# The opening of a fused attention and FFN kernel: image lines of the first two pairs summed on VectorE, first value products set behind the last image line, fp32 dummies in place of fp16 ones

## The chip, the cores and the metric

The kernel runs on one core of a Trainium2 chip. The metric is the device time of one execution in microseconds (us); a profile's span leaves out about 1.8 us of it.

## The reference

```python
B, C, Hh, Ww = (4, 128, 384, 32)              # q: B x 12288 x 128, kv: an image B x 384 x 32 x 128
kv_pool = kv.reshape(B, H//4, 4, W//4, 4, C).mean(axis=(2, 4))
k = v = kv_pool.reshape(B, -1, C) @ w_sr      # 768 keys per batch
a = softmax(q @ k.T / sqrt(C));  x = a @ v    # then a gated FFN, d_ff = 1536:
out = (maximum(x @ w_gate, 0) * (x @ w_val)) @ w_out
```

## The kernel before

The main loop takes 512 queries (a tile) at a time and keeps TensorE full: scores, value products, the two FFN projections and the output product of different tiles are interleaved. In front of it stands an opening that has to pool and project the first batch's image while it arrives. The image comes as three pairs of key chunks with four lines (512 KB each) per pair. A line is pooled by being transposed into one PSUM bank, where the transposes add up, or by being added to another line on VectorE.

```python
def fill(n):                                   # dummies, to raise TensorE's clock (full at 7.66 us)
    for _ in range(n):
        nc.tensor.matmul(idle, ident16, filler, start=True, stop=True)
fill(8)
def values(k, jc, half): ...                   # 2 products of 129 columns into x_banks[k, half]
def attend(k, pair): ...                       # values for both chunks and halves of a pair: 8 products
def turn_add(chunk, lines, first=False): ...   # fp32 transposes adding into kv_Ts[chunk]
def add_lines(pair): ...                       # VectorE: line 0 + line 1, 1024 elements per partition
...
for dh in range(3):                            # pair 0: all four lines on TensorE
    for h in range(2):
        turn_add(h, line(0, dh, h), first=dh == 0)
...
nc.gpsimd.tensor_copy(gate, line(2, 2)[:, 0, 0, 0:1])   # holds these loads until line 2 of pair 2
for own in (slice(0, D_FF // 2), slice(D_FF // 2, D_FF)):
    nc.gpsimd.dma_start(wv16[:, own], moe_w_val[:, own])
    nc.gpsimd.dma_start(wg16[:, own], moe_w_gate[:, own])
q_load(1)                                      # queries of tiles 4 to 7
q_turn(1)                                      # their transpose, a DMA
nc.gpsimd.dma_start(wo16, ...)
for h in range(2):
    turn_add(4 + h, line(2, 3, h), first=h == 0)        # the last image line
```

The query transposes of the following groups (`q_turn`, one per four tiles) and the transposes of the attention results (`x_turn`) are DMAs of the same queue.

The softmax here doesn't subtract the row's maximum and nothing guards it: scores larger than these inputs give would overflow.

Of the kernel before, what the change touches and what calls it, by code (L numbers as in the profile page):

```python
# [10 lines left out]
FP16 = mybir.dt.float16  # L11
AF = mybir.ActivationFunctionType
ALU = mybir.AluOpType
# [3 lines left out]
def kernel(  # L17
# [23 lines left out]
    nc = tc.nc  # L41
# [5 lines left out]
    NJC = J // 128  # L47
# [7 lines left out]
    GRP = 4  # L55
# [8 lines left out]
    const = ctx.enter_context(tc.tile_pool(name="const", bufs=1))  # L64
# [4 lines left out]
    def bank(shape, dtype=FP32):  # L69
        return psum.tile(shape, dtype, tag="bank", name="bank_ps")  # L70
# [53 lines left out]
    def qT_of(k):  # L124
        s0 = (k % GRP) * NS
        return qTs[k // GRP][:, s0 : s0 + NS, :].rearrange("c s p -> c (s p)")
# [31 lines left out]
    def turn_add(chunk, lines, first=False):  # L158

        if first:  # L160
            kv_Ts[chunk] = bank([128, 128])
        for i in range(lines.shape[1]):
            nc.tensor.matmul(  # L163
                kv_Ts[chunk], lines[:, i], ident, is_transpose=True,
                start=first and i == 0, stop=False, skip_group_check=True,
            )

    def turn_end(chunk, lines, engine=nc.vector):
        turn_add(chunk, lines)
        if chunk % 2 == 0:  # L170
            kv_Ts["pair"] = work.tile([128, 2, 128], FP32, tag="kvT", bufs=2, name="kvT")
        kvT = kv_Ts["pair"][:, chunk % 2]
        if engine is nc.scalar:
            nc.scalar.copy(kvT, kv_Ts[chunk])
        else:
            nc.vector.tensor_copy(kvT, kv_Ts[chunk])
        kv_Ts[chunk] = kvT

    def project_chunk(jc, engine=nc.vector):
        pr = bank([128, 128])  # L180
        nc.tensor.matmul(pr, w_sr_f32, kv_Ts.pop(jc), start=True, stop=True)  # L181
        if engine is nc.scalar:
            nc.scalar.mul(kv16[:, 0, jc, 0:C], pr, 1.0 / (r * r))  # L183
        else:
            nc.vector.tensor_scalar(kv16[:, 0, jc, 0:C], pr, 1.0 / (r * r), None, op0=ALU.mult)
# [9 lines left out]
    def turn_values(b, pair):  # L195
        vt = bank([128, 2, 128], FP16)
        for h in range(2):
            nc.tensor.transpose(vt[:, h], kv16[:, b, 2 * pair + h, 0:C], ident16)
        nc.vector.tensor_copy(kv16[:, b, 2 * pair : 2 * pair + 2, C : 2 * C], vt)
# [26 lines left out]
    def scores(k, jc):  # L226
        if jc == 0:
            aTs[k] = work.tile([128, NJC, T], FP16, tag="aT", bufs=4, name="aT")
        s_ps = bank([128, T])
        nc.tensor.matmul(s_ps, kv16[:, k // NST, jc, 0:C], qT_of(k), start=True, stop=True)  # L230
        nc.scalar.activation(aTs[k][:, jc, :], s_ps, AF.Exp, scale=qk_scale)  # L231

    def values(k, jc, half):
        if jc == 0:
            x_banks[k, half] = bank([128, 2, C + 1])
            if half == 0:
                x16s[k] = work.tile([128, NS, C], FP16, tag="x16", bufs=3, name="x16")
        x_ps = x_banks[k, half]
        for i in range(2):
            s = 2 * half + i  # L240
            nc.tensor.matmul(  # L241
                x_ps[:, i, :], aTs[k][:, jc, s * 128 : (s + 1) * 128],
                kv16[:, k // NST, jc, C : 2 * C + 1],
                start=(jc == 0 and i == 0), stop=(jc == NJC - 1), skip_group_check=True,
            )
# [150 lines left out]
    ident = const.tile([128, 128], FP32)  # L396
    make_identity(nc, ident)
    ident16 = const.tile([128, 128], FP16)
# [8 lines left out]
    for pair in range(1, NJC // 2):  # L407
        kv_load(0, pair)

    filler = const.tile([128, 512], FP16)  # L410
    nc.vector.memset(filler, 1.0)
    warm = const.tile([128, 1], FP32)
    nc.vector.memset(warm, 0.0)
    nc.scalar.activation(warm, warm, AF.Exp)
# [6 lines left out]
    idle = bank([128, 512])  # L421

    def fill(n):
        for _ in range(n):
            nc.tensor.matmul(idle, ident16, filler, start=True, stop=True)

    fill(8)

    def attend(k, pair):
        for jc in (2 * pair, 2 * pair + 1):  # L430
            for half in range(2):
                values(k, jc, half)

    def line(pair, dh, h=slice(0, 2)):
        return kv_in[0, pair][:, dh, h]

    def add_lines(pair):
        s2 = work.tile([128, 2, r, C], FP32, tag="kv_s2", bufs=2, name="kv_s2")
        nc.vector.tensor_tensor(s2, line(pair, 0), line(pair, 1), op=ALU.add)
        return s2  # L440

    def add_pixels(s2):
        s1 = work.tile([128, r, C], FP32, tag="kv_s1", bufs=2, name="kv_s1")
        s1 = s1.rearrange("p (h i) c -> p h i c", h=2)
        nc.vector.tensor_tensor(s1, s2[:, :, 0:2], s2[:, :, 2:4], op=ALU.add)
        return s1

    def scores_of(k, pair):
        for jc in (2 * pair, 2 * pair + 1):
            scores(k, jc)  # L450

    for dh in range(3):
        for h in range(2):
            turn_add(h, line(0, dh, h), first=dh == 0)
    for h in range(2):
        turn_end(h, line(0, 3, h), (nc.vector, nc.scalar)[h])
    for h in range(2):
# [11 lines left out]
    scores_of(2, 0)  # L469
    scores_of(3, 0)  # L470

    s1 = add_pixels(add_lines(1))
    attend(0, 0)
    for h in range(2):
        turn_add(2 + h, line(1, 2, h), first=True)
    for h in range(2):
        turn_add(2 + h, s1[:, h])
    for h in range(2):
        turn_end(2 + h, line(1, 3, h), nc.scalar)
    for h in range(2):  # L480
        for half in range(2):
            values(1, h, half)
        project_chunk(2 + h, nc.scalar)
    s2 = add_lines(2)
    scores(0, 2)
    values(2, 0, 0)
    scores(0, 3)
    scores(1, 2)
    scores(1, 3)
    values(2, 1, 0)  # L490
    scores_of(2, 1)
    nc.vector.tensor_tensor(s2[:, 0], s2[:, 0], line(2, 2)[:, 0], op=ALU.add)
    turn_values(0, 1)
    s1 = add_pixels(s2)
    turn_add(5, line(2, 2, 1), first=True)
    attend(0, 1)

    gate = const.tile([128, 1], FP32)
    nc.gpsimd.tensor_copy(gate, line(2, 2)[:, 0, 0, 0:1])
# [6 lines left out]

    for h in range(2):
        turn_add(4 + h, line(2, 3, h), first=h == 0)
    for h in range(2):
        turn_end(4 + h, s1[:, h], (nc.vector, nc.scalar)[h])  # L510
    scores(3, 2)
    for h in range(2):
        for half in range(2):
            values(1, 2 + h, half)
        project_chunk(4 + h, (nc.vector, nc.scalar)[h])
    scores_of(0, 2)
    turn_values(0, 2)
    for jc in (2, 3):
        values(2, jc, 0)
    scores_of(1, 2)  # L520
    attend(0, 2)
    for half in range(2):
        keep_sums(0, half)
# [6 lines left out]
    for jc in range(NJC - 2):  # L530
        values(2, jc, 1)
    late = [(2, 5), (3, 4), (3, 5)]
    left = {2: [(2, jc, half) for half in range(2) for jc in range(NJC - 2, NJC)]}
    for step, k, half in ((4, 3, 0), (7, 3, 1)):
        left[step] = [(k, jc, half) for jc in range(NJC // 2)]
        left[step + 1] = [(k, jc, half) for jc in range(NJC // 2, NJC)]
# [5 lines left out]
    for k in range(LAG, last + 1):  # L542
# [6 lines left out]
        for step in range(NFB):  # L549
            kO, kF = k - LAG - 1, k - LAG  # L550
            half, i = divmod(step // 2, NJC // 2)
# [47 lines left out]
            if b < B:  # L599
# [4 lines left out]
                pair, odd = divmod(at - 4, 2)  # L604
# [7 lines left out]
                pair, odd = divmod(at - 6, 2)  # L612
# [35 lines left out]
```

## Time and profile before

| | before |
|---|---|
| time, median of 3 | 1033.91 us (1033.89 to 1033.99) |
| span of the profile | 1031.3 us |
| start of the last product of TensorE | 1027.65 us |
| first value projection of the main loop | 30.30 us |
| first output product | 38.40 us |
| first query transpose, issue and landing | 33.06 and 37.42 us |

### The profile page before, as it was taken

What the parts mean: (1) busy time and instruction counts of PE and PEld (TensorE: products, weight loads), DVE (VectorE), ACT (ScalarE), POOL (GpSimd) and SP (SyncE); (2) the same over time, 40 slices, a digit from 0 to 9 for tenths busy, and PEclk for the clock granted to TensorE, in tenths of its full rate; (3) what the DMA queues carried; (4) which work ended last, traced back from release to release, by engine and by line L of the source; (5) the groups of instructions that cost most, each with busy time, mean ns of one, the idle gap of its engine ahead of it and who ended that gap; (6) DMA issues with size and microseconds to landing.
All of it is one profiled execution on the core that took longest, in us unless ns stands there. A gap on an engine that the chain in (4) does not pass through costs nothing.

```text
span 1031.3 us, 20032 instructions
## 1 busy us (share of the span) xinstructions
PE 1024.4 (99%) x6580; PEld 546.0 (53%) x6580; DVE 910.0 (88%) x1671; ACT 908.8 (88%) x1745; POOL 279.4 (27%) x287
## 2 busy tenths in 40 slices
PE   8999999999999999999999999999999999999998
PEld 6555555555555555555555555555555555555555
DVE  3889899998989898998889898989888898989898
ACT  4988888889888889888888898888888988888987
POOL 2212146521211125642212121664121221111110
PEclk9999999999999999999999999999999999999999
DMA  8836396462542547836345157573652434513222
GB/s 305 122 57 76 90 195 144 79 93 42 82 69 48 80 120 162 169 53 90 52 68 86 33 84 151 131 173 57 85 73 46 73 54 65 87 32 65 34 40 54
DMA packets 328824, 93.34 MB, mean 91 GB/s; under 512 B 308496, under 2 KB 321936, under 8 KB 328720
## 3 DMA queue, kind: packets, MB, share of 16 engines
q1 hardware_dynamic: 313488, 78.69, 38.7%
q0 software_dynamic: 14944, 13.24, 10.9%
q8 instruction: 51, 0.84, 0.4%
q14 instruction: 53, 0.43, 0.1%
q10 hardware_dynamic: 288, 0.13, 0.0%
HBM read 53.94 MB, written 26.35 MB: 78 GB/s over the span
## 4 chain that ended last, share of the span: by engine, by line
PE 98%; ACT 1%; DMA 1%; SPq 0%; DVE 0%; issue 0%; ACTq 0%
PE bank_ps L279 24%; PE bank_ps L290 24%; PE bank_ps L314 23%; PE bank_ps L241 13%; PE bank_ps L230 12%; PE bank_ps L300 1%; DMA parts<-in_kv_dram 1%; PE bank_ps L163 1%; ACT aT L231 0%; PE bank_ps L189 0%; PE bank_ps L181 0%; SPq L139 0%; ACT val L283 0%; ACT kv L183 0%; PE bank_ps L119 0%
## 5 line engine op out<-in xcount | busy, mean ns | idle before, releaser
L293 DVE SCALAR_TENSOR_TENSOR hT<-bank_ps,val 128x512 f16<-128x512 f32 x1152 | 757.9, 686 | 91.1 <-ACT val L283 70.5
L283 ACT CAST val<-bank_ps 128x512 f16<-128x512 f32 x1152 | 677.8, 589 | 102.5 <-PE bank_ps L279 100.5
L279 PE MATMUL bank_ps<-xT,wv 128*128 128x512 f16 x1152 | 436.6, 379 | 0.2 <-DVE rinv L249 0.2
L290 PE MATMUL bank_ps<-xT,wg 128*128 128x512 f16 x1152 | 436.6, 379 | 0.0
L314 PE MATMUL bank_ps<-hT,wo 128*128 128x512 f16 x1116 | 423.0, 379 | 0.0
L231 ACT ACTIVATE aT<-bank_ps 128x512 f16<-128x512 f32 x576 | 345.8, 604 | 1.0 <-PE bank_ps L230 1.0
L324 POOL TENSOR_SCALAR o_sb<-o_t 128x512 f32<-128x512 f32 x93 | 138.3, 1487 | 694.1 <-DVE rinv L249 660.0
L241 PEld LDWEIGHTS <-aT 128*128 128x128 f16 x2304 | 177.3, 98 | 133.1 <-issue 0.9
L241 PE MATMUL bank_ps<-kv,aT 128*128 128x129 f16 x2304 | 223.6, 220 | 0.0
L230 PE MATMUL bank_ps<-qT,kv 128*128 128x512 f16 x576 | 217.3, 379 | 0.4 <-DVE qT L122 0.2
L279 PEld LDWEIGHTS <-wv 128*128 128x128 f16 x1152 | 112.7, 98 | 132.7 <-issue 0.3
L290 PEld LDWEIGHTS <-wg 128*128 128x128 f16 x1152 | 112.7, 98 | 67.3
L314 PEld LDWEIGHTS <-wo 128*128 128x128 f16 x1116 | 109.2, 98 | 65.9 <-issue 0.2
L230 PEld LDWEIGHTS <-kv 128*128 128x128 f16 x576 | 56.1, 98 | 67.6 <-issue 0.8
L257 DVE TENSOR_TENSOR x<-bank_ps,rinv 128x256 f16<-128x256 f32 x190 | 80.6, 424 | 6.6
L322 DVE STREAM_TRANSPOSE o_t<-bank_ps 128x512 f32<-128x512 f32 x93 | 65.7, 706 | 0.0
L86 POOL DMA_DIRECT2D q<-in_q_dram x88 | 48.3, 556 | 0.3 <-issue 0.3
L148 POOL TENSOR_TENSOR s<-parts 128x512 f32<-128x512 f32 x36 | 44.8, 1265 | 0.0
L249 DVE RECIPROCAL rinv<-bank_ps 128x2 f32<-128x2 f32 x192 | 27.9, 146 | 0.8 <-PE bank_ps L241 0.8
L150 POOL TENSOR_TENSOR s<-s 128x512 f32<-128x512 f32 x18 | 22.8, 1266 | 1.4
L152 POOL TENSOR_TENSOR c<-s 128x256 f32<-128x256 f32 x18 | 13.0, 724 | 1.4
L300 PEld LDWEIGHTS <-hT 128*128 128x128 f16 x144 | 10.1, 98 | 5.8
(53 smaller groups left out, 94.6 us busy)
## 6 DMA issues: line engine op xcount, KB each, us to landing
parts<-in_kv_dram SPq DMA_DIRECT2D x48, 512.0 KB, 6.5
out_dram<-o_sb SPq DMA_DIRECT2D x353, 64.0 KB, 2.2
q<-in_q_dram POOLq DMA_DIRECT2D x88, 128.0 KB, 4.6
xT<-x SPq DMA_TRANSPOSE x94, 2.4
out_dram<-o_sb SPq DMA_DIRECT2D x80, 16.0 KB, 1.5
placed<-blocks SPq DMA_DIRECT2D x9, 128.0 KB, 1.8
kvT<-placed SPq DMA_DIRECT2D x36, 32.0 KB, 1.9
q<-in_q_dram SPq DMA_DIRECT2D x2, 512.0 KB, 8.0
```

The source lines that it names most:

```text
L86: nc.gpsimd.dma_start(q16[32 * j : 32 * (j + 1)].rearrange("t (i s) c -> t i s c", i=GRP), rows[j])
L230: nc.tensor.matmul(s_ps, kv16[:, k // NST, jc, 0:C], qT_of(k), start=True, stop=True)
L231: nc.scalar.activation(aTs[k][:, jc, :], s_ps, AF.Exp, scale=qk_scale)
L241: nc.tensor.matmul(x_ps[:, i, :], aTs[k][:, jc, s * 128 : (s + 1) * 128], kv16[:, k // NST, jc, C : 2 * C + 1], start=(jc == 0 and i == 0) ...
L257: nc.vector.tensor_tensor(x16s[k][:, 2 * half : 2 * half + 2, :], x_ps[:, :, 0:C], rinv.to_broadcast([128, 2, C]), op=ALU.mult,)
L279: nc.tensor.matmul(va_ps, wv16[:, fb * 128 : (fb + 1) * 128], xTs[k], start=True, stop=True)
L283: nc.scalar.copy(val, va_ps)
L290: nc.tensor.matmul(g_ps, wg16[:, fb * 128 : (fb + 1) * 128], xTs[k], start=True, stop=True)
L293: nc.vector.scalar_tensor_tensor(hTs[k][:, fb, :], g_ps, 0.0, vals.pop((k, fb)), op0=ALU.max, op1=ALU.mult)
L314: nc.tensor.matmul(o_banks[k], wo16[:, fb, :], hTs[k][:, fb, :], start=fb == 0, stop=fb == NFB - 1)
L322: nc.vector.transpose(o_t, o_banks.pop(k))
L324: nc.gpsimd.tensor_scalar(o_sb.rearrange("t j s c -> t s j c"), o_t.rearrange("t (s j c) -> t s j c", s=NS, j=4), 1.0 / X_SCALE**2, None, ...
```

## The change

It is meant to bring the last image line into TensorE sooner. TensorE issues fewer instructions before that line (94 products with 94 weight loads, where there were 134 and 134), so that its instruction queue does not fetch its next block while the line is on its way (before, that packet ran from 20.95 to 22.04 us and the line landed at 23.09), and value products that stood before the line are moved behind it. The core of the diff:

```diff
-            nc.tensor.matmul(idle, ident16, filler, start=True, stop=True)
-    fill(8)
+            nc.tensor.matmul(
+                idle, ident, ident[:, 0:1].to_broadcast([128, 512]), start=True, stop=True
+            )
+    fill(4)
 ...
-    for dh in range(3):
-        for h in range(2):
-            turn_add(h, line(0, dh, h), first=dh == 0)
+    s1 = add_pixels(add_lines(0))
+    for h in range(2):
+        turn_add(h, line(0, 2, h), first=True)
+    for h in range(2):
+        turn_add(h, s1[:, h])
 ...
-    s1 = add_pixels(add_lines(1))
+    s2 = add_lines(1)
+    for h in halves:
+        add_third(1, s2, h)
+    s1 = add_pixels(s2, halves)
 ...                                     (pair 1: line 2 no longer on TensorE)
     for h in range(2):
-        for half in range(2):
-            values(1, h, half)
         project_chunk(2 + h, nc.scalar)
-    values(2, 0, 0) ... values(2, 1, 0)  (between the scores)
-    attend(0, 1)                         (ahead of the last line)
 ...                                     (behind the last line)
+    attend(0, 1)
+    project_chunk(5, nc.scalar)
+    for half in range(2):
+        values(1, 0, half)
 ...
+    left = {1: [(2, jc, 0) for jc in range(NJC - 2)], 2: ...}   # 8 products into step 1 of the loop
```

More of the change, by code (lines that the diff above doesn't have):

```diff
@@ L408 @@
         kv_load(0, pair)
-    filler = const.tile([128, 512], FP16)
-    nc.vector.memset(filler, 1.0)
     warm = const.tile([128, 1], FP32)
@@ L440, in add_lines, with add_pixels @@
         return s2
-    def add_pixels(s2):
+    def add_pixels(s2, halves=(slice(0, 2),)):
         s1 = work.tile([128, r, C], FP32, tag="kv_s1", bufs=2, name="kv_s1")
         s1 = s1.rearrange("p (h i) c -> p h i c", h=2)
-        nc.vector.tensor_tensor(s1, s2[:, :, 0:2], s2[:, :, 2:4], op=ALU.add)
+        for h in halves:
+            nc.vector.tensor_tensor(s1[:, h], s2[:, h, 0:2], s2[:, h, 2:4], op=ALU.add)
         return s1
@@ L470, with add_third @@
     scores_of(3, 0)
-    s1 = add_pixels(add_lines(1))
+    halves = (slice(0, 1), slice(1, 2))
+    def add_third(pair, s2, h):
+        nc.vector.tensor_tensor(s2[:, h], s2[:, h], line(pair, 2)[:, h], op=ALU.add)
+    s2 = add_lines(1)
+    for h in halves:
+        add_third(1, s2, h)
+    s1 = add_pixels(s2, halves)
     attend(0, 0)
     for h in range(2):
-        turn_add(2 + h, line(1, 2, h), first=True)
+        turn_add(2 + h, line(1, 3, h), first=True)
     for h in range(2):
-        turn_add(2 + h, s1[:, h])
+        turn_end(2 + h, s1[:, h], nc.scalar)
     for h in range(2):
-        turn_end(2 + h, line(1, 3, h), nc.scalar)
-    for h in range(2):
-        for half in range(2):
-            values(1, h, half)
         project_chunk(2 + h, nc.scalar)
     s2 = add_lines(2)
-    scores(0, 2)
-    values(2, 0, 0)
-    scores(0, 3)
-    scores(1, 2)
-    scores(1, 3)
-    values(2, 1, 0)
-    scores_of(2, 1)
-    nc.vector.tensor_tensor(s2[:, 0], s2[:, 0], line(2, 2)[:, 0], op=ALU.add)
+    for k in range(GRP - 1):
+        scores_of(k, 1)
+    add_third(2, s2, halves[0])
+    s1 = add_pixels(s2, halves)
     turn_values(0, 1)
-    s1 = add_pixels(s2)
     turn_add(5, line(2, 2, 1), first=True)
-    attend(0, 1)
     gate = const.tile([128, 1], FP32)
@@ L508 @@
         turn_add(4 + h, line(2, 3, h), first=h == 0)
-    for h in range(2):
         turn_end(4 + h, s1[:, h], (nc.vector, nc.scalar)[h])
+    project_chunk(4)
     scores(3, 2)
-    for h in range(2):
-        for half in range(2):
-            values(1, 2 + h, half)
-        project_chunk(4 + h, (nc.vector, nc.scalar)[h])
+    attend(0, 1)
+    project_chunk(5, nc.scalar)
+    for half in range(2):
+        values(1, 0, half)
     scores_of(0, 2)
     turn_values(0, 2)
-    for jc in (2, 3):
-        values(2, jc, 0)
+    for half in range(2):
+        values(1, 1, half)
     scores_of(1, 2)
+    attend(1, 1)
     attend(0, 2)
@@ L532 @@
     late = [(2, 5), (3, 4), (3, 5)]
-    left = {2: [(2, jc, half) for half in range(2) for jc in range(NJC - 2, NJC)]}
+    left = {
+        1: [(2, jc, 0) for jc in range(NJC - 2)],
+        2: [(2, jc, half) for half in range(2) for jc in range(NJC - 2, NJC)],
+    }
     for step, k, half in ((4, 3, 0), (7, 3, 1)):
```

## The prediction

> **What bounds the kernel now.** I read the page's chain of waits first, then the table of windows, then TensorE's timeline and the DMA view of the opening.
>
> ```profile
> span 1031.3 us, 20032 instructions
> PE 98%; ACT 1%; DMA 1%; SPq 0%; DVE 0%; issue 0%; ACTq 0%
> ```
>
> TensorE carries the chain for 98% of the span. The columns of the next table are stretch, length, then busy time of each engine.
>
> ```profile
> 22.70:30.30 7.60, 7.35 (x78) 5.89 (x79) 3.07 (x12) 4.69 (x10) 4.30 (x8) 1.00 1.04 140
> 30.30:40.00 9.70, 9.66 (x70) 5.33 (x71) 9.09 (x21) 9.29 (x21) 0.00 (x0) 1.00 0.94 137
> 40.00:1020.00 980.00, 980.00 (x6221) 516.35 (x6219) 883.00 (x1612) 878.70 (x1683) 272.42 (x269) 1.00 0.49 84
> ```
>
> From 40 us on TensorE never pauses (980.00 of 980.00), and the change leaves that part alone. Every matmul start from there is a sum of fixed costs, so whatever the change moves the start of the dense stretch by, it moves the end by. "Busy" hides short gaps, because a matmul's modelled end overlaps the next; I compared starts instead. At full clock a 128x512 fp16 product follows its forerunner by 0.216 us, a 129-column one by 0.057, a 128-column fp16 transpose by 0.056, an fp32 transpose by 0.109, and a whole fp32 projection (two instructions) takes about 0.275. What exceeds these is idle time.
>
> The opening waits for 12 image lines of 512 KB and two query blocks. In the trace's record of landings (the last of 16 semaphore increments) the lines of pair 0 are complete at 5.19, 6.46, 8.49, 9.75, the queries at 11.03, 12.31, pair 1 at 13.59, 14.86, 16.15, 17.43, pair 2 at 18.71, 19.98, 21.27 and 23.09 us. The pace is 1.28 us per transfer, but the last one needed 1.82. TensorE around it:
>
> ```profile
> 22.19 0.27 PE L198 MATMUL bank_ps<-ident,kv 128*128 128x128 f16 x2
> 22.69 0.66 PE L163 MATMUL bank_ps<-ident,parts 128*128 128x128 f32 x4 [0.22 <-ACT aT L231]
> 23.18 0.62 PE L241 MATMUL bank_ps<-kv,aT 128*128 128x129 f16 x8
> 23.63 1.04 PE L163 MATMUL bank_ps<-ident,parts 128*128 128x128 f32 x8
> ```
>
> The last line's transposes (23.63) start 0.54 us after it landed. TensorE had waited for a PSUM bank held by an exponential, then did four transposes of line 2 and eight value products, and only then came to the last line. Why that line was late shows in the queues of 20.9 to 21.0 us:
>
> ```profile
> q8 instruction: 1, 0.02, 68.2%
> q1 hardware_dynamic: 7, 0.02, 42.3%
> ```
>
> One 16 KB packet of instructions starts at 20.95 us and lasts 1.09 us, on a machine otherwise full of 4 KB image packets. The image packets beside it end at 22.48 us; at the old pace about 0.5 us earlier.
>
> [...] 51 packets, 0.84 MB, on queue 8, for TensorE's 13,160 loads and products, one per some 20 us of the dense part. [...] Here fp16 dummies go every 0.427 us, fp32 transposes every 0.213 until 7.6 us and every 0.109 after; the granted clock becomes full at 7.66. [...] The trace has 1.22 us for 1024 elements and 0.69 for 512[...].
>
> **The change part by part.**
>
> *Dummies.* Eight fp16 products become four fp32 ones. From the projections I take an fp32 product as two instructions at two cycles a column, so 512 columns cost 2 x 0.427 at full clock and 2 x 0.853 = 1.71 us at half. Four take up to 6.8 us from about 1.36 (the fp32 identity is ready 0.3 us before its fp16 copy) to 8.2, or near 8.0 if the clock rises at 7.66. The first TensorE work of pair 0 becomes line 2, landed at 8.49. No gain, no loss, still eight products.
>
> *Pair 0.* Lines 0 and 1 go to VectorE: 1.22 + 0.69 from 6.5 to about 8.4. TensorE does 20 transposes instead of 32; line 3's start about 9.9 instead of 9.79, and end within 0.1 us of where they did. Nothing for the end.
>
> *Pair 1.* Line 2 also goes to VectorE. From 15.24: sum 1.22, two half adds of 0.69 (line 2 landed at 16.15), two pixel halves of about 0.42, so the halves are ready near 18.25 and 18.65. TensorE does 12 transposes instead of 20, but now ends on the pixel sums: both ScalarE copies, projections and the first exponential come 0.3 to 0.4 us later (20.45 instead of 20.07), the sixth ends near 23.4. It was in the shadow of the transfers and stays there.
>
> *Count.* Before the last line TensorE now has 8 dummies, 20+12 pair transposes, 8 projection instructions, 16 query transposes, 14 scores, 8 values, 4 value transposes, 4 transposes of line 2: 94 products, 188 with their loads, instead of 134 and 268. In the kernel before the fetch started when 239 instructions had started, so I expect it after TensorE passes the last line. Then that line keeps the pace: 21.27 + 1.28 = 22.55, and its transposes start at 22.60, as TensorE has nothing else left and, with three fewer accumulators alive, banks enough. **First term: 23.63 - 22.60 = 1.03 us earlier.**
>
> *Work moved behind the line, up to the main loop.* attend(0,1) is 8 products and values(1,0..1) 8 more; of values(2,...) 4 leave this stretch (into the loop). 8 + 8 - 4 = 12 x 0.057 = **0.68 us later.** The 4 of k=2 issued before the line until now also go into the loop.
>
> *Idle time in that stretch.* Before, 23.63 to 30.30 is 6.67 us, of which my paces account for about 5.81: 0.86 idle, at the second score (0.27), a value product (0.15), the first value projection (0.32), and small ones. After, the stretch holds 6.49 us of work. Following it through: the DVE copy of chunk 4 at 23.55, its projection issued right behind chunk 5's transposes, eight value products between the two projections, scores of chunk 5 at 25.74 (0.09 idle), the exponentials of (1,5) done at 27.9, x_turn after VectorE's normalisation (0.18 idle), first projection after the xT copy (0.20 idle): about 0.47. **0.39 us earlier.** The main loop starts at 22.60 + 6.49 + 0.47, near 29.56 instead of 30.30.
>
> *In the loop.* values(2,0..3,0) is 8 products in step 1: 8 x 0.057 = **0.46 us later.** But the first steps have idle time: ScalarE alternates evictions and exponentials from 30.7 to 33.8, and TensorE pauses 0.21 and 0.04 us for a bank.
>
> ```profile
> 32.27 0.50 ACT aT L231
> 32.77 0.48 ACT val L283
> 33.26 0.51 ACT aT L231
> 33.76 0.04 issue
> 33.81 0.22 PE bank_ps L241
> ```
>
> The inserted products lie in that pause: **0.25 us earlier.**
>
> Sum: 1.03 - 0.68 + 0.39 - 0.46 + 0.25 = 0.53 us earlier, 0.05% of the span. 1033.91 - 0.53 = 1033.4 us.
>
> **The rivals.** (a) The fetch is not dodged. Against it: TensorE's stream is some 60 instructions behind at 20 us. For it: TensorE may prefetch so far ahead that standing at the line does not hold it back. The line lands at 23.09, the first term falls to about 0.5, and the time stays at 1033.9 to 1034.0. (b) The moved products are paid in full, because the remaining idle time comes from ScalarE's and VectorE's chains, which the change also shifts: 1.03 - 0.68 - 0.46 = -0.11, so 1034.0. Against it: most of the old idle is a wait for a chunk that the change finishes earlier relative to the work at hand. (c) Pair 1's longer VectorE chain holds banks past 22.6: the late exponentials end at 23.4, and one bank too few would delay the last line's transposes by one exponential (0.48), leaving about nothing. Against it: only two accumulators are alive there instead of five. (d) More is gained: with ScalarE less behind, the small pauses up to 39 us (0.16) vanish as well, giving 1033.2. (e) The fp32 dummies run longer than I take them or leave the clock low, and pair 0 is late: the queries (12.31) set what follows, so about 1 us is free before it hurts.
>
> **Range and chances.** The three runs before span 0.1 us and the dense part adds nothing, so the spread is that of the opening: -0.1 to +1.1 us. I predict 1033.4 us, 1032.8 to 1034.0 for 8 in 10. Two per cent is 20.7 us, and all of the opening's idle time from the first dummy on is under 9 us, so within 2% has 0.98, faster 0.01, slower 0.01.
>
> **What would show it.** The last line's transposes at about 22.6 instead of 23.63; the instruction packet after 22.5 instead of at 20.95; 36 fp32 transposes read straight from image lines where there were 60, and 12 from sums where there were 8; the first value projection near 29.6 instead of 30.30; TensorE dense from 40 us as before. I am wrong if the packet still lies before the last line's end, if TensorE waits for a bank at 22.6, or if the steady part shows idle time.

The packet delays the line; the traces show the delay, not its mechanism. The 0.42 us for a sum of 256 elements, as an estimate, follows from the line through the two lengths measured before (1.22 us for 1024 elements, 0.69 for 512), and the four such sums in the opening of the changed kernel took 0.42.

## More of the kernel before

The prediction shows the chain, the windows and the critical piece of the opening. One more view matters for what came of it: TensorE's timeline where the fifth tile starts (start, busy time, engine, line, operation). Line 230 at 38.93 us is its first score, the first reader of the DMA-transposed queries.

```profile
38.40 0.38 PE L314 MATMUL bank_ps<-hT,wo 128*128 128x512 f16 x1
38.72 0.38 PE L279 MATMUL bank_ps<-xT,wv 128*128 128x512 f16 x1
38.93 0.38 PE L230 MATMUL bank_ps<-qT,kv 128*128 128x512 f16 x1
39.21 0.38 PE L290 MATMUL bank_ps<-xT,wg 128*128 128x512 f16 x1
```

No wait is printed beside it, so the first query transpose's landing at 37.42 us (its issue was at 33.06) was early enough, with 1.5 us to spare. A transfer that is in time leaves no mark in the chain of waits; its slack has to be looked up.

## The result, and the profile after

| us | before | changed |
|---|---|---|
| median of 5 runs | 1033.91 (1033.40 to 1034.15) | 1033.66 (1033.31 to 1034.32) |
| span of the profile | 1031.3 | 1031.9 |

The ratio of the two is 0.9999, with a 95% interval of 0.9984 to 1.0014 (here and below a ratio is the mean time of one kernel's fast runs over that of the other's of the same rounds, so not quite the ratio of the medians). The median is inside the predicted range, but that range (1032.8 to 1034.0) also holds the kernel before at 1033.91, and the predicted gain of 0.05% is smaller than the interval. The times alone settle nothing; the traces do.

The last line first: TensorE's timeline of the changed kernel, answering to the four lines of the prediction.

```profile
20.98 0.28 PE L198 MATMUL bank_ps<-ident,kv 128*128 128x128 f16 x2
21.23 0.65 PE L163 MATMUL bank_ps<-ident,parts 128*128 128x128 f32 x4
22.25 0.63 PE L163 MATMUL bank_ps<-ident,parts 128*128 128x128 f32 x4 [0.36 <-ACT aT L231]
```

The third row is the last line, at 22.25 instead of 23.63 us. By the record of landings it landed at 22.11, 1.23 us after the line before it (20.88); before, that distance was 1.82. The packet of instructions now starts at 22.41, when the last image packet has ended (21.66):

```profile
q0 software_dynamic: 7, 0.01, 15.9%
q8 instruction: 1, 0.02, 6.6%
```

These are the DMA queues of 21.7 to 22.6 us: the instructions (q8) meet only the first packets of the FFN weights (q0), no image (q1). The profile names an exponential (ACT aT) as what ended TensorE's wait, though the line landed at nearly the same moment. In all the profiles below where TensorE waits here, the transposes start 0.13 or 0.14 us after the landing, also in two (a_pad and only_values) where it comes 1.1 and 1.2 us later than the pace; so it is the line, and the name is that of a neighbour in time. It was a near thing: the exponential had ended 0.07 to 0.09 us before the transposes, where 0.05 or 0.06 us is the distance in before, whose transposes of line 2 do wait for a bank.

Then the table of windows, the same stretches as in the prediction (length, then busy time of PE, PEld, DVE, ACT, POOL):

```profile
22.70:30.30 7.60, 7.54 (x82) 5.72 (x81) 3.38 (x13) 5.57 (x12) 3.92 (x7) 1.00 1.06 150
30.30:40.00 9.70, 8.49 (x73) 5.04 (x72) 8.90 (x20) 8.66 (x20) 0.09 (x1) 1.00 1.19 139
40.00:1020.00 980.00, 979.91 (x6217) 516.07 (x6216) 882.17 (x1609) 878.73 (x1682) 272.80 (x269) 1.00 0.49 84
```

The first stretch is fuller (7.54 where it was 7.35). The second, full before (9.66 of 9.70), lacks 1.2 us, and even the long dense one lacks 0.09. The page's chain shows who took it:

```profile
PE 95%; DMA 4%; POOL 0%; SPq 0%; issue 0%; ACT 0%; ACTq 0%
PE bank_ps L279 24%; PE bank_ps L290 24%; PE bank_ps L314 23%; PE bank_ps L241 12%; PE bank_ps L230 11%; DMA q<-in_q_dram 1%; DMA parts<-in_kv_dram 1%; PE bank_ps L300 1%; DMA xT<-x 1%; DMA qT<-q 1%; PE bank_ps L189 0%; SPq L139 0%; POOL q L86 0%; POOL wv L502 0%; POOL wg L503 0%
```

The query transpose and the load ahead of it (qT<-q, q<-in_q_dram) stand in a chain in which they did not appear before. In the timeline:

```profile
37.47 0.38 PE L314 MATMUL bank_ps<-hT,wo 128*128 128x512 f16 x1
37.70 0.38 PE L279 MATMUL bank_ps<-xT,wv 128*128 128x512 f16 x1
39.29 0.39 PE L230 MATMUL bank_ps<-qT,kv 128*128 128x512 f16 x1 [1.21 <-DMA qT<-q]
```

TensorE reached the fifth tile 0.93 us sooner (first output product 37.47 instead of 38.40; 0.40 of it because the second query block landed earlier in this execution, as the clock below shows) and then stood for a query transpose that landed at 39.24, 6.29 us after its issue at 32.95. Before, it was issued at 33.06 and took 4.36. From start to start that costs 1.37 us beyond a product's own 0.22; the 0.09 us that the dense stretch lacks are part of a second wait, of 0.25 us for an attention result's transpose at 184.35 us.

**A common clock for all profiles.** The transfers of the opening do not start equally early in each execution: over the 14 profiles the second query block lands at 11.6 to 12.8 us, with no relation to the kernel. I therefore count from that landing: A, to the first output product; R, from there to the start of TensorE's last product. From that start to the end of the span it is 3.64 to 3.66 us in all of them. So span = landing + A + R + 3.65.

| profile | landing | first value projection | A | R | query transpose |
|---|---|---|---|---|---|
| before | 12.31 | 17.99 | 26.09 | 989.25 | 4.36 |
| before, again | 12.19 | 17.99 | 26.09 | 989.26 | 4.43 |
| changed | 11.91 | 17.24 | 25.56 | 990.75 | 6.29 |
| changed, again | 12.31 | 17.23 | 25.54 | 989.80 | 5.80 |
| changed, third | 12.82 | 17.23 | 25.54 | 989.96 | 6.04 |

A repeats to 0.02 us. The change took 0.54 us out of the opening, and R gave back 0.55 to 1.50 in these three profiles. R at its lowest, in profiles below without any stall, is 989.11. That is 0.14 under before, whose small pauses behind the first output product (0.10 and 0.06 us, the rows at 38.72 and 39.21 above) are gone in the changed kernel; so without a stall the change would be worth 0.54 + 0.14 = 0.68 us.

### The profile page after: what moved, and what is told of

The parts are those of the page before. It is cut to its first block, busy times and chain, and to the rows that moved or that the text cites. A ratio compares the mean times of both kernels' runs of the same rounds, so it can differ in the third digit from the quotient of the medians.

```text
span 1031.9 us, 20001 instructions
## 1 busy us (share of the span) xinstructions
PE 1022.9 (99%) x6560; PEld 543.8 (53%) x6560; DVE 913.4 (89%) x1676; ACT 909.4 (88%) x1745; POOL 279.9 (27%) x287
## 4 chain that ended last, share of the span: by engine, by line
PE 95%; DMA 4%; POOL 0%; SPq 0%; issue 0%; ACT 0%; ACTq 0%
PE bank_ps L279 24%; PE bank_ps L290 24%; PE bank_ps L314 23%; PE bank_ps L241 12%; PE bank_ps L230 11%; DMA q<-in_q_dram 1%; DMA parts<-in_kv_dram 1%; PE bank_ps L300 1%; DMA xT<-x 1%; DMA qT<-q 1%; PE bank_ps L189 0%; SPq L139 0%; POOL q L86 0%; POOL wv L502 0%; POOL wg L503 0%
```

## The experiments

Two theories. **F**: TensorE's instructions come in packets of 16 KB, one for every 256 (51 packets for 13,189 instructions in before's profile, those that only wait counted too; when a packet started, 172 to 239 of a block of 256 had started), and the moment is set, roughly, by the count of instructions passed. With 40 fewer instructions in the opening the second packet (near 33.4 us before, 35.1 in the changed kernel) falls into the query transpose, which it slows, and later packets into later transposes. **N**: the stall was chance and has nothing to do with the change. A rival for the cause inside F was **W**: the transpose is slow because of other transfers beside it.

### a_repeat, a_repeat2: the changed kernel unaltered

> The changed kernel once more, unaltered, for a second profile. Theory F (the second instruction packet of TensorE, at its 448th instruction, falls into the query transpose): packet near 35 us, query transpose 6 us or more from issue to landing, first score of the fifth tile near 39.3 with about 1.3 us of idle TensorE, time within 0.4 us of the kernel before. Rival N (the stall of the first profile was chance): no stall near 39 us, span near 1030.5, time about 1 us under the kernel before.

Measured: 1033.81 us (1033.09 to 1034.68), before of the same job 1033.30 (1032.72 to 1034.35), ratio 1.0004 (0.9991 to 1.0016). The packet at 35.92 us, the query transpose 5.80 us, but the score waited for it by less than 0.1 us: it landed at 38.33, just in time. The stall came elsewhere:

```profile
182.98 0.38 PE L314 MATMUL bank_ps<-hT,wo 128*128 128x512 f16 x1
183.78 0.39 PE L279 MATMUL bank_ps<-xT,wv 128*128 128x512 f16 x1 [0.43 <-DMA xT<-x]
```

That is a wait for an attention result's transpose. The trace's packets show an instruction packet at 179.69 us, inside the query transpose issued at 177.01 (8.21 us; 4.95 and 5.09 in the two profiles of before, where no packet fell into it), and the attention results' transpose stands in the same queue. So half of my expectation failed: the place and size of the stall, the transpose's 6 us or more, and the time (0.51 us over before, where I had said within 0.4). The cause held. The loss is not one wait of 1.3 us but a wait here or there.

> The changed kernel for a third profile, beside the reordered one below. Counted from the landing of the second query block: first value projection after 17.24 us, first output product after 25.55 (before: 17.99 and 26.09 in two profiles). Theory F: second instruction packet at 35 to 36 us inside the query transpose, which takes 5.5 us or more (4.4 where the packet misses it), TensorE idle there or behind a later transpose by 0.1 to 1.7 us in all; time within 0.5 us of before. Rival N: the query transpose under 5 us, time 0.5 under before.

Measured: 1033.57 us (1032.17 to 1033.91), before 1032.99 (1032.66 to 1033.63), so 0.58 over it in the median where I had allowed 0.5; ratio 1.0001 (0.9988 to 1.0013). The packet at 36.42, query transpose 6.04 us, and both stalls at once, 0.39 us at the fifth tile and 0.44 near 184 us. The first projection (17.23) and output product (25.54) came out as said. Two of its five executions took 1032.17 and 1032.56 us, so a changed kernel that meets no stall is possible; which executions met one cannot be read from times.

### b_repeat: the kernel before unaltered

> The kernel before once more, for a second profile. Counted from the landing of the last line but one, the first value projection follows after 9.0 us as in its first profile (8.27 in both profiles of the changed kernel). Theory F: the second instruction packet near 33.5 us ahead of the query transpose's data, no stall near 39 us. Rival N (its first profile was a lucky one, and it usually stalls too): packet at 34 to 37 us, query transpose over 5.5 us, TensorE idle near 39 us.

Measured: 1033.12 us, before 1033.10, ratio 1.0001. The packet at 32.80 us, ahead of the transpose's issue (33.09); transpose 4.43 us; no idle TensorE from 40 us on. N is out as far as two profiles of before and three of the changed kernel can tell.

### a_pad: 40 more instructions in front of everything

```diff
-    fill(4)
+    fill(2)
+    for _ in range(24):
+        nc.tensor.matmul(idle[:, 0:128], ident16, ident16, start=True, stop=True)
```

> The changed kernel with two of its four fp32 dummies exchanged for 24 short fp16 ones, so that 40 more instructions pass TensorE ahead of everything. Theory F: the first packet is back near 21 us and the last image line lands about 0.5 us later after its forerunner (1.7 to 1.8 us instead of 1.23), so the main loop starts 0.3 to 0.6 us later than in the changed kernel; the second packet comes near 33.5, before the query transpose moves data, which then lands 4.4 us after issue; no stall near 39 us; net 0.5 to 1.0 us under the changed kernel. Rival W (the transpose is slow because the load of the output weights or the other transposes lie beside it): the stall near 39 us stays and the time is 0.3 to 0.6 us over the changed kernel.

Measured: 1032.92 us (1032.88 to 1033.72), before 1033.30, ratio 0.9998 (0.9984 to 1.0011). First packet at 20.52, the last line 2.44 us after its forerunner, so the delay was larger than I expected; TensorE's wait says so too:

```profile
20.91 0.66 PE L163 MATMUL bank_ps<-ident,parts 128*128 128x128 f32 x4
23.12 0.63 PE L163 MATMUL bank_ps<-ident,parts 128*128 128x128 f32 x4 [1.56 <-DMA parts<-in_kv_dram]
```

The second packet at 32.81, and in the DMA view of 32 to 40 us the query transpose is as quick as before:

```profile
q0 software_dynamic: 923, 0.23, 29.4%
xT<-x SPq DMA_TRANSPOSE x2, 3.2
qT<-q SPq DMA_TRANSPOSE x1, 4.4
```

In the changed kernel the same view reads

```profile
q0 software_dynamic: 860, 0.22, 27.7%
xT<-x SPq DMA_TRANSPOSE x2, 3.4
qT<-q SPq DMA_TRANSPOSE x1, 6.3
```

The weights (q0) beside it are about as many in both, and there were more of them in before (1220 packets), where the transpose was quick as well. The first attention transpose comes later in a_pad (issued 3.2 us after the query transpose, 2.6 in the changed kernel), so a_pad alone leaves it as a rival; a_padlast below has it at 2.5 us and a quick query transpose, and with that W is out. A is 26.75, 1.2 us worse, R is 989.11, without a stall: the opening's gain is undone and more, and the later loss with it.

### a_padlast: the 40 instructions where TensorE waits anyway

```diff
     turn_add(5, line(2, 2, 1), first=True)      # shortened: written out, its bank twice as wide
+    for _ in range(20):
+        nc.tensor.matmul(wide[:, 128:129], ident16, ident16[:, 0:1],
+                         start=False, stop=False, skip_group_check=True)
```

> The changed kernel with 20 one-column products (40 instructions) set right ahead of the last line's transposes, where TensorE waits anyway. Theory F: the first packet is asked for so late that the line's data is already through (line lands 1.2 to 1.3 us after its forerunner), the last line's transposes start 0 to 0.5 us later than in the changed kernel, the second packet comes near 33 us and misses the query transpose, which lands about 4.4 us after issue; no stall near 39 us; time 0.5 to 1.2 us under the changed kernel, about 1032.7. Rival: the first packet hits the last line after all (1.7 us or more), or the stall stays; then the time is that of the changed kernel or more.

Measured: 1032.54 us (1032.30 to 1034.80), before 1033.10, ratio 0.9997 (0.9984 to 1.0010). TensorE's timeline:

```profile
21.49 0.66 PE L500 MATMUL bank_ps<-ident,parts 128*128 128x128 f32 x4
21.98 0.64 PE L505 MATMUL bank_ps<-ident 128*128 128x1 f16 x20
22.50 0.63 PE L163 MATMUL bank_ps<-ident,parts 128*128 128x128 f32 x4
```

The 20 dummies fit into the wait; the last line starts 0.14 us after its landing (22.36) as without them. First packet at 22.26, second at 32.71, ahead of the transpose, which takes 4.46 us; no stall at the fifth tile; A is 25.57, the full gain. This is the clean test: nothing but a count of instructions moved, and the query transpose went from 5.8 to 6.3 us back to 4.5. A later packet (682.57 us, inside the query transpose issued at 680.08) was followed by a stall of 0.52 us near 686 us (R is 989.64), and one execution at 1034.8 makes the interval wide: better in the median by 0.56 us, not beyond noise.

### a_qearly, a_qearly2, b_qearly: the second query group ahead of half of the weights

```diff
     for own in (slice(0, D_FF // 2), slice(D_FF // 2, D_FF)):
         nc.gpsimd.dma_start(wv16[:, own], moe_w_val[:, own])
         nc.gpsimd.dma_start(wg16[:, own], moe_w_gate[:, own])
-    q_load(1)
-    q_turn(1)
+        if own.start == 0:
+            q_load(1)
+            q_turn(1)
```

> The changed kernel with the load and transpose of the second query group issued ahead of the second half of the FFN weights. Theory F: the transpose ends before the packet of 35 us, no stall near 39 us, the main loop's start unchanged (29.2), time 1.0 to 1.4 us under the changed kernel, about 1032.5. Rival H (the second half of the weights now comes too late, as it lands up to 2.6 us later): a wait for wv or wg near 34 us of up to 1 us, and no gain.

Measured: 1032.38 us (1031.52 to 1032.94), before 1033.30, ratio 0.9989 (0.9976 to 1.0001). The stall is gone and the weights are in time, but not in the way I expected: the transpose was issued at 30.65 and took 7.4 us, beside the weights and with the packet (35.94) inside it, landing at 38.02, shortly before its score:

```profile
38.11 0.38 PE L279 MATMUL bank_ps<-xT,wv 128*128 128x512 f16 x1
38.33 0.38 PE L230 MATMUL bank_ps<-qT,kv 128*128 128x512 f16 x1
```

It helps by starting 2.3 us earlier, not by ending ahead of the packet. A is 25.54, R 989.11: here the opening's gain reaches the end, 0.69 us less than in before for the two together.

> The changed kernel with the second query group ahead of the second half of the weights, once more. If its gain was real: 0.5 to 1.2 us under before and 0.5 to 1.4 under the changed kernel of this job, no idle TensorE near 39 us, first value projection 17.23 us after the second query block. If it was chance: within 0.3 us of both.

Measured: 1032.59 us (1032.09 to 1033.26), before 1032.99, the changed kernel of that job 1033.57; ratio to before 0.9995 (0.9982 to 1.0007). A is 25.55, R 989.36 (landing 38.30, 0.1 us late; a second small stall of 0.13 us near 183 us). The best version that I found: 0.9 and 0.4 us under before in the medians of two jobs (I had asked for 0.5 in the second), with both intervals reaching past 1, so the times do not show it faster than before.

> The kernel before with the same reordering. Theory F: in its profile there was no stall at the query transpose, so nothing is gained: within 0.2 us of the kernel before. If instead the unprofiled executions of the kernel before (0.3 to 1 us slower than the profiled one) stall there, it is 0.3 to 0.8 us faster.

Measured: 1033.24 us, before 1033.30, ratio 0.9999 (0.9986 to 1.0012). Nothing gained, as expected of a kernel that does not stall there. Its profile had a late opening (with the instruction packet at 20.93 the line before the last was complete only at 23.08, 3.0 us after its forerunner) and one stall of 0.38 us near 688 us behind a packet at 683.8: the kernel before is not free of such meetings either.

### only_values: the value products alone

The changed kernel with the dummies and the pair sums of before.

> Only the value products are moved behind the last line; dummies and pair sums as before. Its 192nd TensorE instruction is the same as before, so by theory F the first packet starts near 21 us and the last line lands 1.7 to 1.8 us after its forerunner, not 1.23. TensorE is ready by then, so the first value projection follows 8.8 to 8.9 us after the landing of the last line but one (before 9.03, changed 8.27), and with 8 more products in the loop nothing is left: time within 0.3 us of before, or more if the second packet meets the query transpose. Rival V (moving the products is the whole gain, the count does nothing): 8.3 us.

Measured: 1033.71 us (1033.49 to 1033.85), before 1033.10, ratio 1.0004 (0.9990 to 1.0018). The packet at 20.21, the last line 2.33 us after its forerunner; the first value projection 9.37 us after that forerunner. My 8.8 to 8.9 was worked out with a delay of 1.82; with 2.33 it is that much more. The time missed my 0.3 us: the profile shows one more stall, 0.61 us near 687 us, behind a packet at 682.99. Rival V (8.3) is out: without the lower count TensorE is ready early and stands waiting for the line.

### only_sums and sums_dummies: the pair sums without the value products

```diff
 only_sums: pair 0 and pair 1 as in the changed kernel, the rest as before
 sums_dummies: the same, and
-    fill(8)            # fp16
+    fill(4)            # fp32
```

> Only the pair sums are moved to VectorE; values and dummies as before. 40 TensorE instructions fewer before the last line, the 192nd near 20.5 us, so the first packet starts after 22 us and the last line lands 1.23 to 1.3 us after its forerunner. But TensorE comes to it late as before, behind the value products and the bank: first value projection 8.8 to 9.1 us after the landing of the last line but one. The second packet shifts to about 35 us, into the query transpose, which then takes 6 us: TensorE idle 0.2 to 0.6 us near 39 us, time 0 to 0.5 us over before.

Measured: 1035.43 us (1034.67 to 1036.15), before 1033.10, ratio 1.0021 (1.0007 to 1.0035). A clear miss: 2.3 us slower. The last line came 1.23 us after its forerunner with the packet at 22.44, as expected; but the granted clock was full only at 14.12 us (7.66 in before), and pair 0 ran at half rate:

```profile
1.71 3.60 PE L425 MATMUL bank_ps<-filler,ident 128*128 128x512 f16 x8 [1.71 <-POOL ident L399]
8.55 1.97 PE L163 MATMUL bank_ps<-ident,parts 128*128 128x128 f32 x8 [3.24 <-DMA parts<-in_kv_dram]
10.31 1.06 PE L163 MATMUL bank_ps<-ident,kv_s 128*128 128x128 f32 x4
```

Eight transposes take 1.97 us, where they took 1.09 in before. With lines 0 and 1 on VectorE TensorE has nothing to do for 3.24 us after its dummies. A is 28.75, 2.7 us over before, which is the loss; with the opening so late the second packet (38.06) came when the query transpose's data was through (4.37 us), so there was no stall.

> Pair sums on VectorE and fp32 dummies, the value products where they were. Theory C: clock full by 7.7 us, the 2 us lost with the sums alone are back. Theory F: last line 1.23 us after its forerunner, first packet after 22 us; but TensorE comes to the line as late as before, so the first value projection follows the second query block after 17.8 to 18.2 us (before 17.99, changed 17.24). Second packet near 35 us in the query transpose: it takes 5.5 us or more, TensorE idle 0.2 to 0.6 us near 39 us. Time 0 to 0.6 us over before. Rival: the early landing alone brings 17.5 or less.

Measured: 1033.44 us (1033.06 to 1033.83), before 1032.99, ratio 1.0003 (0.9988 to 1.0018). The fp32 dummies bring the 2 us back: clock full at 5.67 us. The last line 1.22 us after its forerunner (the packet at 21.52, as the last data passed), and TensorE comes to it late, at 24.01 us, behind a bank and the value products:

```profile
22.57 0.27 PE L198 MATMUL bank_ps<-ident,kv 128*128 128x128 f16 x2
23.07 0.65 PE L163 MATMUL bank_ps<-ident,parts 128*128 128x128 f32 x4 [0.22 <-ACT aT L231]
23.56 0.62 PE L241 MATMUL bank_ps<-kv,aT 128*128 128x129 f16 x8
24.01 1.04 PE L163 MATMUL bank_ps<-ident,parts 128*128 128x128 f32 x8
```

First value projection at 18.41, so 0.42 later than before and 0.2 beyond my range: pair 1's longer way over VectorE delays its exponentials, and with five accumulators alive a bank waits for them. The query transpose met its packet (37.26) and took 6.04 us, but the later kernel lost only 0.08 us by it. So the sums alone cost 0.4 us, the values alone buy nothing while the packet holds the line, and only together they give 0.54.

### a_fp16: the changed kernel with the dummies of before

> The changed kernel with the eight fp16 dummies of before. Theory C (with lines 0 and 1 on VectorE, TensorE has nothing from 5.1 to 8.5 us and the clock does not rise; the fp32 dummies are there to fill this): granted clock full only near 14 us as in the run with the sums alone, the opening at half rate, first value projection 1.5 to 2.7 us later than in the changed kernel, time 1.3 to 2.7 us over it. Rival[...]: clock full at 5.5 to 7.7 us, time as the changed kernel.

Measured: 1034.22 us (1032.57 to 1035.15), before 1032.99, the changed kernel of that job 1033.57; ratio to before 1.0009 (0.9995 to 1.0023). The clock full at 14.13 us, the first value projection at 18.91 (1.68 us later than in the changed kernel), A 27.22; R 989.11, without a stall at the later fifth tile. The time is 0.65 us over the changed kernel, half of the least that I had expected, because the changed kernel's own R carried stalls of 0.85 us in that job's profile. The late clock came in both profiles that had the sums and the fp16 dummies and in none of the other twelve (5.6 to 7.7 us). One execution of four was as quick as 1032.57, so it need not be so in every one.

## Why the prediction was right or wrong, point by point

The time lay in a range wide enough to hold the kernel before too, so that says little, and that the median fell 0.25 us under before's is within the noise. The sum of the opening was right to a few hundredths; the sentence that carried it to the end of the kernel was not.

- **First term, the line at the old pace:** right. The packet came after the line in every profile of the unaltered changed kernel (22.41, 25.01, 26.26 us), the line kept the pace (1.22 to 1.25), and a_pad put both back. From the second query block its transposes start after 10.34 us instead of 11.32, so 0.98 us earlier for the 1.03 forecast. Note that in before the late line was not the last thing that TensorE waited for: it landed after 10.78 and 11.12 us in the two profiles, and its transposes started after 11.32 and 11.33. That is why only_values, which makes TensorE ready early, and sums_dummies, which brings the line early, gain nothing alone.
- **Moved products, saved idle time, main loop 0.74 us earlier:** measured 0.75 (17.99 to 17.24 from the second query block).
- **Loop: 0.46 later for the inserted products, 0.25 earlier by the pause they fill:** measured together, A is 0.53 to 0.55 us shorter, and I had 0.53. The pause of 0.21 us at 33.6 us is gone.
- **"whatever the change moves the start of the dense stretch by, it moves the end by":** wrong, the step that failed. I took the dense stretch as bound by TensorE's work alone because TensorE never paused in it, and did not ask how much slack its transfers had. The first query transpose had 1.5 us. The change spent 0.54 of that by reaching the fifth tile sooner, and 1.4 to 1.9 us more by shifting the second instruction packet into the transpose. In three profiles R grew by 0.55 to 1.50 us, as much as the opening gave or more. My list of what would show me wrong named it, as idle time in the steady part; none of my rivals was this one.
- **Rival a** (packet not dodged) and **b** (products paid in full) did not happen. **Rival d** (the small pauses up to 39 us, 0.16 us, vanish as well) did, hidden by the stall: it is the 0.14 us of R above. **Rival c** is what sums_dummies shows, where the value products keep their banks; in the changed kernel the bank came free by a few hundredths of a us before the line.
- **Dummies, "no gain, no loss":** right for the change as a whole, but the reason was missing. They ran from 1.36 to 7.7 us, two instructions of 0.853 us each at half clock, as worked out. What I overlooked is that the sums on VectorE take away the transposes that kept TensorE busy from 5.2 us; without longer dummies the opening loses 1.7 us (a_fp16, clock full at 14.13 us instead of 6.74). My rival e feared that they leave the clock low; it is their absence that does.

What remains open: how one 16 KB packet stretches a transpose by 1.4 us or more. In the changed kernel's trace 394 of the transpose's 256-byte packets start in the half microsecond from 35.0 us and 60 in the next. The median one takes 18 ns, but 22 of those started between 35.41 and 35.74 all end at 37.05 to 37.08, 0.9 us after the instruction packet (35.06 to 36.18), and then the flow resumes. Such packets of more than 0.8 us, all ending together, stand in each of the five slow transposes of the last paragraph of this section and in none of the six quick ones. This suggests that the transpose stops as a whole for what the instruction packet holds up; no run takes it apart. Other instruction packets (q14, 8 KB) fall into the five slow ones as well, but in three of them only after the flow had resumed (37.94 us in the changed kernel), and b_qearly's transpose was slow without one. In before's whole trace the attention results' transposes took 2.44 us in the median of the 81 without a TensorE packet inside and 3.92 us in the 13 with one (a longer transpose is also likelier to meet one).

That a changed count of instructions moves the packet off the transpose is shown by a_pad and a_padlast. The count does not fix the moment: the second packet started between 0.3 us before and 2.0 us after TensorE's 448th instruction over the 14 profiles. That meetings account for the whole scatter of single times is not shown.

Over the 11 profiles in which the load of the queries was not brought forward the time of the first query transpose falls into two groups without overlap: 4.36 to 4.46 us in the six where no packet fell into its data, 5.70 to 6.29 in the five where one did. The three with the earlier load, all with a packet inside, took 6.8 to 7.4 us.

## What to carry to other kernels

Before you carry a gain at the front of a full engine's work to the end, list the transfers that the later work reads and their slack: the moment of need moves forward, the transfer need not (here TensorE came to the fifth tile 0.93 us sooner, and its query transpose was issued 0.11 us sooner). An engine's own instruction fetch is a transfer too; here its moment followed roughly from a count, so removing or adding instructions moved it onto or off a sensitive DMA (40 fewer: the second packet from 33.43 to 35.06 us; 40 added again: 32.81 in a_pad, 32.71 in a_padlast), and an idle slot was a place to set the count at almost no cost (a_padlast: A 25.57 where it was 25.54 to 25.56). When runs scatter by more than the effect, count from an event that the change cannot touch and compare stretches, not ends.

## What else the traces show

- An instruction packet in the way. One packet delayed the last image line by 0.6 to 1.2 us (1.82 to 2.44 us after its forerunner, 1.22 to 1.25 without) and a query transpose from 4.4 to between 5.7 and 6.3 us. When it comes: in before's profile TensorE's 192nd instruction (those that only wait counted too) started at 18.06 us and the packet at 20.95, amid the image traffic; the 448th at 32.90 and the packet at 33.43; in the dense part packets came when 172 to 228 of a block's 256 had started.
- A transpose's time beside other packets. The query transpose took 4.3 us alone and 8 to 10 us in most later groups; the one near 178 us took 7.0 to 8.2 us in the profiles where an instruction packet fell into it and 4.7 to 6.6 where none did.
- The clock under transposes. In before, with fp16 dummies to 5.1 us and transposes alone from 5.23, it was full at 7.66, 5.95 us after the first dummy; in only_sums, after a pause, with transposes from 8.55 and projections from 12.87, at 14.12, 5.57 us after they began. No run has transposes alone, so what they do by themselves is not shown.
